# Fetching a second weight piece earlier, and one matrix product moved ahead of a group, in a fused retention and MLP kernel

## Chip, cores, metric

One core of a Trainium2 chip. The metric is the device time of one execution in microseconds (us). Several executions are timed; one of them is taken with the profiler, and its trace is what the views below are read from. The span in a profile (666.3 us for the kernel before) is about 1.7 us shorter than the time of the same execution.

## The reference, cut to what matters

```python
# attention: (batch 4, heads 8, seq 768, head_dim 64), retention with a decay per head
state = gamma * state + k[t] (outer) v[t]
y[t]  = scale * q[t] @ state
# bridge to x: (3072 tokens, 512), then
h = x @ w_in                      # (512, 2048)
g = np.maximum(0.01 * h, h)       # leaky relu
return g @ w_out                  # (2048, 512)
```

The weights arrive as float64 and the kernel converts them itself. The sequence is cut into six groups of 128 positions; a group with its 4 batches has 512 tokens, in two halves of 256 (batches 0 and 1, batches 2 and 3).

## The kernel before, where the change and the argument touch it

Each weight piece (512 KB) is loaded and converted by three activations on ScalarE (`powers`) and three operations on VectorE (`mantissas`). Loads go out on one queue, in this order:

```python
    load_qk(0, 0); load_v(0, 0)      # qk is 512 KB, v 256 KB
    load_qk(0, 1); load_v(0, 1)
    load_piece(0)
    load_qk(0, 2); load_v(0, 2)
    load_piece(1)
    load_piece(2)
    load_piece(3, words)
    # ... qk and v of batch 3, the k's, group 1
```

The first products (`direct`, tiles `d`) multiply x by pieces 0 to 3 as they become ready. TensorE executes this order:

```python
    values(0, 1)              # tiles yp
    score(0, 2)               # needs qk of batch 2; tiles ap
    keep_busy(3)              # three bf16 filler matmuls, tile idle
    next(steps)               # direct product on piece 0 (8 matmuls)
    next(steps)               # direct product on piece 1
    values(0, 2)
    # ... (order on TensorE; the loads and conversions between are cut)
```

Later, matrix products run in the Strassen-Winograd form: seven products of blocks instead of eight, each 8 matmuls, collected in four accumulators A to D:

```python
        which = [("M1", "A", 0, 0), ("M6", "B", 5, 5), ("M5", "C", 4, 4), ("M4", "D", 3, 6),
                 ("M2", "A", 2, 2), ("M7", "B", 1, 1), ("M3", "C", 6, 3)]
        for m, bank, sa, sb in which:
            # first use of a letter: psum.tile([128, 2, N], FP32, tag="ff", bufs=4)
            # ... 8 matmuls of weight block sa and x (sb < 4) or t (sb - 4)
            takes(m, ps)      # ScalarE or VectorE reads the accumulator
            yield
```

M1 and M2 of the hidden layer read only the first token half of x. The others need `differences(x, t)`, hence both halves. VectorE frees B with M7's add and C with M3's. PSUM, the memory in which matmuls accumulate, holds four `ff` tiles of one bank and two `att` tiles of two (`two_banks` in the code). The end of the start-up:

```python
    scored_later(2); scored_later(3)          # scores and masks of group 1
    last_sum(0); next_mantissas()
    products_in_turn(2)                       # reads, values, state of batches 2, 3
    next_powers(); run(steps, {})             # last direct product
    tokens_taken(1, 2, x1); tokens_taken(1, 3, x1)
    differences(x1, t1)
    state_taken(1, 2); state_taken(1, 3)
    run(hidden(1, 0, x1, t1, *parts[1][1:]),
        {0: [next_mantissas], 1: [lambda: differences(*parts[0][1:])],
         2: [next_powers], 3: [lambda: add_sums(1)]})
    # then output(0, ...), output(1, ...), hidden(0, u=1), ...
```

## Time and profile before

| | before |
|---|---|
| time, first three runs | 668.04, 668.18, 670.51 us |
| profiled span, mean granted clock of TensorE (PE) | 666.3 us, 1.000 |
| PE busy | 659.5 us, 99% |
| VectorE (DVE) busy, ScalarE (ACT) busy | 56%, 26% |
| PE's waits in the waits view, whole span | 3.5 us |

The granted clock is the share of TensorE's full clock that the profile shows as granted. With PE busy for 99% of the span, the change looks for its saving in PE's idle time, and every wait that the waits view lists lies in the first 42 us. A timeline line gives the start, the length, the engine, the source line, what it writes and reads, how many instructions are merged, and in brackets the idle time ahead with what ended it. The lines themselves stand in the prediction.

### The profile page before, as it was taken

The page shows a single profiled execution, that of the slowest core. Times are in us where ns is not written, and L with a number is a line of the kernel's source. Part 1 is how long each engine was busy: PE and PEld are TensorE (multiplying, and loading weights), DVE is VectorE, ACT ScalarE, POOL GpSimd, SP SyncE. Part 2 cuts the span into 40 slices and gives each one's busy share as a digit, 9 for nine tenths or more (in the row PEclk, how much of TensorE's full clock was granted, in tenths as well). Part 3 has the DMA queues.
Part 4 walks back from the last instruction along what each step waited for, and adds up shares of the span by engine and source line. Part 5 has one row for each costly group of instructions (what it writes and reads, how often), then busy time and mean ns, then how long its engine had stood idle before and what let it go on. Part 6 is the DMA issues. An engine that isn't in the chain of part 4 may idle for free.

```text
span 666.3 us, 10403 instructions
## 1 busy us (share of the span) xinstructions
PE 659.5 (99%) x4505; PEld 572.8 (86%) x4505; DVE 374.3 (56%) x570; ACT 176.0 (26%) x322; POOL 20.1 (3%) x22
## 2 busy tenths in 40 slices
PE   8999999999999999999999999999999999999998
PEld 4888888888888888888888888888888888888886
DVE  5789869889888676315543613563431444431342
ACT  4854555255261002211201311210221220221210
POOL 0000000000000111000000100100100000000000
PEclk9999999999999999999999999999999999999999
DMA  8930312312312453003002200301300001000001
GB/s 321 399 107 32 126 64 64 126 65 89 133 67 85 167 191 127 1 0 128 1 31 83 77 1 1 127 1 64 127 1 0 2 0 40 23 1 1 0 1 63
DMA packets 15757, 48.92 MB, mean 73 GB/s; under 512 B 1752, under 2 KB 2008, under 8 KB 15712
## 3 DMA queue, kind: packets, MB, share of 16 engines
q1 hardware_dynamic: 15696, 48.24, 20.2%
q8 instruction: 35, 0.57, 0.3%
q14 instruction: 10, 0.08, 0.0%
q10 hardware_dynamic: 16, 0.02, 0.0%
HBM read 41.97 MB, written 6.29 MB: 72 GB/s over the span
## 4 chain that ended last, share of the span: by engine, by line
PE 97%; DMA 1%; SPq 1%; DVE 1%; ACT 0%; issue 0%; DVEq 0%
PE B_o L412 12%; PE A_o L412 12%; PE C_o L412 12%; PE C_h L412 12%; PE B_h L412 12%; PE A_h L412 12%; PE D_o L412 6%; PE D_h L412 6%; PE yp L193 3%; PE ap L165 3%; PE d L434 2%; PE yp L184 2%; DMA raw<-in_weights_dram 1%; PE yp L208 1%; SPq L134 0%; PE sums L208 0%
## 5 line engine op out<-in xcount | busy, mean ns | idle before, releaser
L412 PE MATMUL A_h<-x,w 128*128 128x256 f32 x368 | 86.9, 379 | 0.0
L412 PEld LDWEIGHTS A_h<-x,w 128*128 128x128 f32 x368 | 69.9, 190 | 9.5
L412 PE MATMUL A_o<-g,w 128*128 128x256 f32 x288 | 68.0, 379 | 0.0
L447 ACT ACTIVATE g<-g 128x512 f32<-128x512 f32 x69 | 42.0, 630 | 91.3 <-DVE g L361 91.3
L412 PEld LDWEIGHTS A_o<-g,w 128*128 128x128 f32 x288 | 54.7, 190 | 7.4
L452 ACT COPY m<-A_h 128x512 f32<-128x512 f32 x23 | 13.4, 582 | 141.3 <-PE A_h L412 101.6
L361 DVE TENSOR_TENSOR m<-m,B_o 128x512 f32<-128x512 f32 x16 | 10.9, 684 | 63.9 <-PE B_o L412 63.9
L361 DVE TENSOR_TENSOR m<-m,B_h 128x512 f32<-128x512 f32 x23 | 15.7, 684 | 54.7 <-PE B_h L412 54.7
L412 PE MATMUL C_h<-t,w 128*128 128x256 f32 x184 | 44.1, 382 | 0.0
L412 PE MATMUL B_h<-x,w 128*128 128x256 f32 x184 | 44.1, 382 | 0.0
L412 PE MATMUL B_h<-t,w 128*128 128x256 f32 x184 | 43.5, 379 | 0.0
L412 PE MATMUL C_h<-x,w 128*128 128x256 f32 x184 | 43.5, 379 | 0.0
L412 PE MATMUL D_h<-t,w 128*128 128x256 f32 x184 | 43.5, 379 | 0.0
L238 DVE TENSOR_TENSOR x<-yp,dec 128x512 f32<-128x512 f32 x24 | 16.4, 687 | 48.0 <-PE yp L208 34.2
L412 PEld LDWEIGHTS C_h<-t,w 128*128 128x128 f32 x184 | 34.5, 190 | 5.5 <-issue 0.9
L412 PEld LDWEIGHTS B_h<-t,w 128*128 128x128 f32 x184 | 35.0, 190 | 4.8
L412 PEld LDWEIGHTS C_h<-x,w 128*128 128x128 f32 x184 | 35.0, 190 | 4.8
L412 PEld LDWEIGHTS D_h<-t,w 128*128 128x128 f32 x184 | 35.0, 190 | 4.8
L412 PEld LDWEIGHTS B_h<-x,w 128*128 128x128 f32 x184 | 34.5, 190 | 5.1 <-issue 0.3
L364 DVE TENSOR_TENSOR gd<-g,gd 128x512 f32<-128x512 f32 x48 | 35.5, 740 | 1.6
L170 DVE TENSOR_TENSOR am<-ap,mask 128x1024 f32<-128x1024 f32 x24 | 28.5, 1218 | 10.5 <-PE ap L165 10.5
L412 PE MATMUL B_o<-gd,w 128*128 128x256 f32 x144 | 34.0, 379 | 0.0
(118 smaller groups left out, 1020.4 us busy)
## 6 DMA issues: line engine op xcount, KB each, us to landing
raw<-in_weights_dram SPq DMA_DIRECT2D x31, 512.0 KB, 4.2
qk<-in_qk_dram SPq DMA_DIRECT2D x19, 512.0 KB, 3.8
kv<-in_kv_dram SPq DMA_DIRECT2D x17, 512.0 KB, 4.5
out_dram<-o SPq DMA_DIRECT2D x23, 256.0 KB, 2.1
in<-in_qk_dram SPq DMA_DIRECT2D x3, 512.0 KB, 7.7
in<-in_kv_dram SPq DMA_DIRECT2D x3, 512.0 KB, 8.2
kv<-in_kv_dram SPq DMA_DIRECT2D x4, 256.0 KB, 7.3
o_in<-in_qk_dram SPq DMA_DIRECT2D x2, 512.0 KB, 8.7
```

The costliest lines, as they stand in the source:

```text
L165: nc.tensor.matmul(ps[ts(u, 64), j, a, :], lhsT=x[ts(j, 64), 1, a, ts(u, 64)], rhs=x[ts(j, 64), 0, a, :])
L170: nc.vector.tensor_tensor(out=am.rearrange("p j a t -> p (j a) t"), in0=scores[c, b].rearrange("p j a t -> p (j a) t"), in1=mask.unsqueeze ...
L184: nc.tensor.matmul(ps[ts(i, 64), j, m, :], lhsT=st[b][ts(j, 64), a, :], rhs=x[ts(j, 64), 0, a, :], start=(m == 0), stop=False, skip_group_ ...
L193: nc.tensor.matmul(ps[ts(i, 64), j, m, :], lhsT=y[:, 1, 2 * a + j, :], rhs=am[:, j, a, :], start=(c == 0 and m == 0), stop=True, skip_grou ...
L208: nc.tensor.matmul(sp[ts(j, 64), a, :], lhsT=y[:, 0, 2 * a + j, :], rhs=y[:, 1, 2 * a + j, :], start=start, stop=True, skip_group_check=True)
L238: nc.vector.tensor_tensor(out=blocks, in0=ps[:, :, 0 : HP // 2, :], in1=gq, op=ALU.mult)
L361: nc.vector.tensor_tensor(out=out, in0=a, in1=b, op=ALU.add)
L364: nc.vector.tensor_tensor(out=out, in0=a, in1=b, op=ALU.subtract)
L412: nc.tensor.matmul(half, lhsT=block(w, sa)[:, k, ts(i, 128)], rhs=rhs[:, k, :], start=(first and (i == 0 or split) and n == 0 and k == 0), ...
L434: nc.tensor.matmul(banks[r][:, i, :], lhsT=block(2 * u, r + 2 * kh)[:, k, ts(i, 128)], rhs=x[:, 2 * kh + th, k, :], start=(step == 0 and i ...
L447: nc.scalar.activation(g[:, i], g[:, i], AF.Prelu, alpha=0.01)
L452: nc.scalar.copy(out=got["m1"], in_=ps)
```

## The change

The intent is to shorten PE's wait for the second weight piece, and to put work into the hole in which PE waits for a masked score tile.

```diff
     load_piece(0)
+    load_piece(1)
     load_qk(0, 2)
     load_v(0, 2)
-    load_piece(1)
...
-        for m, bank, sa, sb in which:
+        for m, bank, sa, sb in (which[i] for i in order):
...
     scored_later(2)
     scored_later(3)
+    later = hidden(1, 0, x1, t1, *parts[1][1:], order=(0, 4, 1, 2, 3, 5, 6))
+    next(later)
     last_sum(0)
...
-    run(hidden(1, 0, x1, t1, *parts[1][1:]),
-        {0: [next_mantissas], ...
+    run(later, {0: [next_mantissas], ...
```

I call the first hunk part 1 and the rest part 2. In part 2, M1 runs right behind the scores of group 1, and M2 is the first product of what is left.

More of the change, by code (lines that the diff above doesn't have):

```diff
@@ L387, in last_difference, with seven @@
         minus(x[:, 1], x[:, 3], x[:, 1])
-    def seven(tiles, name, takes, takes_half=None):
+    ORDER = (0, 1, 2, 3, 4, 5, 6)
+    def seven(tiles, name, takes, takes_half=None, order=ORDER):
         banks = {}
@@ L440, in direct, with hidden @@
             yield
-    def hidden(c, u, x, t, g, gd):
+    def hidden(c, u, x, t, g, gd, order=ORDER):
         got = {}
@@ L473, in takes @@
                 differences(g, gd)
-        return seven([(2 * u, x, t)], f"h{at}", takes)
+        return seven([(2 * u, x, t)], f"h{at}", takes, order=order)
     def output(c, o, parts, first, final):
@@ L732 @@
     state_taken(1, 3)
-    run(hidden(1, 0, x1, t1, *parts[1][1:]),
-        {0: [next_mantissas], 1: [lambda: differences(*parts[0][1:])],
-         2: [next_powers], 3: [lambda: add_sums(1)]})
+    run(later, {0: [next_mantissas], 1: [lambda: differences(*parts[0][1:])],
+                2: [next_powers], 3: [lambda: add_sums(1)]})
     for u in range(NU):
```

## The prediction

> **What bounds the kernel now.** I read the page first: the matmul engine (PE) is busy 99% of 666.3 us and the chain that ended last is 97% PE. So almost any microsecond taken from PE's idle time is a microsecond of the kernel, and there is very little of it. The second view, who waited for whom with the filter PE, lists all of it over the whole span:
>
> ```profile
> PE d L434 <- DVE w L357: 1.4, 2, 1.0
> PE idle L624 <- DVE t L619: 1.4, 1, 1.4
> PE yp L184 <- DVE am L170: 0.5, 1, 0.5
> PE ap L165 <- DMA qk<-in_qk_dram: 0.2, 1, 0.2
> ```
>
> The columns are total us, times, longest. The change aims at the first row (waits for converted weights) and the third (a wait for a masked score tile); together 1.9 us, 0.3% of the time. That caps the change before any detail. The third view, the timeline of PE in the first 50 us, shows where they lie:
>
> ```profile
> 11.33 1.10 PE L165 MATMUL ap<-o_in 64*64 64x128 f32 x32
> 12.37 0.82 PE L624 MATMUL idle<-t 128*128 128x512 bf16 x3
> 13.58 1.99 PE L434 MATMUL d<-x,w 128*128 128x256 f32 x8 [0.39 <-DVE w L357]
> 16.59 1.99 PE L434 MATMUL d<-x,w 128*128 128x256 f32 x8 [1.01 <-DVE w L357]
> ...
> 39.89 1.05 PE L165 MATMUL ap<-qk 64*64 64x128 f32 x32
> 41.41 0.67 PE L184 MATMUL yp<-in,states 64*64 64x128 f32 x16 [0.47 <-DVE am L170]
> ```
>
> The first number is the start, the second the length. The product on weight piece 1 starts at 16.59, 3.01 us after the one on piece 0, though eight matmuls occupy PE for only 1.92 us (the spacing 16.59 to 18.51). Why it waits is in the timelines of the other two engines:
>
> ```profile
> 13.22 0.66 ACT L334 ACTIVATE w<-raw 128x512 f32<-128x512 uint16 x1 [1.53 <-DMA raw<-in_weights_dram]
> ...
> 15.84 0.69 DVE L357 SCALAR_TENSOR_TENSOR w<-w,z 128x512 f32<-128x512 f32 x1
> ```
>
> ScalarE (ACT) sat idle from 11.69 until piece 1 landed at 13.22; three activations and three VectorE (DVE) operations later, at 16.53, the piece is usable.
>
> [...] from issue 11 on, the queue's own waits show each issue waiting for the landing of the one eight before it, so issue times read as landings: piece 0 at 9.69, qk of batch 2 near 10.97, its v at 11.87, piece 1 at 13.22; 512 KB per 1.28 us, 410 GB/s[...]. [...] the largest idle gap here is 1.4 us and the granted clock is 1.000, so moving a gap of 1 us should not cost clock. [...] The code uses four one-bank tiles (ff) and two two-bank tiles (att)[...]. A new accumulator must therefore wait for VectorE or ScalarE to empty an old one. That becomes my main term.
>
> **Part 1, piece 1 earlier.** Nothing is added or removed; piece 1 (512 KB) overtakes qk (512 KB) and v (256 KB) of batch 2. Estimated landings from the spacing above: piece 1 at 10.97, qk at 12.25, v at 13.2; everything later unchanged.
> - ScalarE goes straight from piece 0 to piece 1 at 11.7 (first activation over at 12.4, second at 13.06, third at 13.7). VectorE finishes piece 0 at 13.52 and needs about 1.95 us (14.58 to 16.53) for piece 1: ready at 15.5 instead of 16.53.
> - But PE's program has the score of batch 2 ahead of the first weight product. It began at 11.33; now it waits for qk until 12.3. It takes 1.04, and three filler matmuls take 0.64 (one alone lasts 0.39 at 9.82, three last 0.82, so each further one adds 0.215). So product 0 starts at 12.3 + 1.04 + 0.64 = 13.98, 0.4 later than before, and product 1 at 13.98 + 1.92 = 15.90.
> - Shift x = 16.59 - 15.90 = **0.69 us**. I checked the consumers down to 41 us: piece 2 (ready 18.9, used 19.9), piece 3 (23.0, used 24.7), decays and later loads (at least 0.7 us ahead of their use, and they aren't moved). I find none that gives x back.
>
> **Part 2, product M1 of hidden(1,0) ahead.** M1 needs only block 0 of the weights and x1[:,0] (first token half, written by 38.8). Its eight matmuls (1.73 us by the spacing in the chain, 47.58 to 49.31) move from after the last direct product to between the scores and the reads of batches 2 and 3. Scores stream 32 matmuls in 0.93 (38.96 to 39.89), so PE is free at 40.82 and the reads come at 41.41: the real hole is 0.59, a little over the 0.47 listed. M1 fills it wholly. M2 becomes the first product of the rest: it also reads only the first half, and it adds into M1's bank, long copied by then. The count of instructions is equal. So on PE alone the gain is 0.69 + 0.59 = **1.28 us**.
>
> **What comes back.** M1 is longer than its hole, so the products of batches 2 and 3 come 1.73 - 0.59 = 1.14 later in PE's order; with x, 0.45 later by the clock. VectorE's tokens_taken, which starts a long burst of work, waits for exactly those. It began at 45.24 and now begins near 45.69, while PE's later stream is 1.28 earlier. VectorE in that stretch, timeline of before:
>
> ```profile
> 45.24 1.29 DVE L238 TENSOR_TENSOR x<-yp,dec 128x512 f32<-128x512 f32 x2 [0.29 <-PE yp L208]
> ...
> 61.94 0.69 DVE L364 TENSOR_TENSOR gd<-g 128x512 f32<-128x512 f32 x1 [0.70 <-ACT g L447]
> ...
> 71.50 0.68 DVE L361 TENSOR_TENSOR m<-m,B_o 128x512 f32<-128x512 f32 x1
> ...
> 73.49 0.68 DVE L361 TENSOR_TENSOR o<-u,C_o 128x512 f32<-128x512 f32 x1
> 75.30 0.69 DVE L361 TENSOR_TENSOR u<-m,B_o 128x512 f32<-128x512 f32 x1 [1.14 <-PE B_o L412]
> ```
>
> From 45.24 to 74.2 it is 27.24 us busy in 29.00 (the table by stretch), and its one listed wait, 0.70 for ScalarE's leaky, follows from VectorE's own add before it. So I take this burst as rigid: all of it moves by +0.45. Its adds free the banks of output(0,0) for output(1,0):
> - B_o is free at 72.18 before, its next use began at 73.32: slack 1.14. Now free at 72.63, plus 0.06 (semaphore, as from 13.52 to 13.58): 72.69, against a wish for 73.32 - 1.28 = 72.04. Wait 0.65.
> - C_o is free at 74.17, next use 75.05: slack 0.88. Now 74.68, against 72.69 + 1.73 = 74.42. Wait 0.26.
> - After that VectorE has its 1.14 idle at 75.3 and over 2 us of slack to the next banks; no more waits.
> Net: 1.28 - 0.65 - 0.26 = **0.37 us**. The same falls out in one step: the end is set by VectorE's burst at C_o, 75.05 - 74.68. It also says that part 2 alone would lose: with x = 0 the release would be 1.14 later, the next use at 75.37, a loss of 0.32; and part 1 alone would gain its whole 0.69.
>
> **Time.** Before, two runs agree at 668.04 and 668.18 (one at 670.51 is an outlier); 668.11 - 0.37 = **667.7 us**.
>
> **Rivals.**
> - *No debt: both holes close and stay closed*, 666.8. For it: VectorE is busy only 56% overall[...]. Against: the burst has no gap before 75.3. It would be right if VectorE's order has slack that I can't see, or if the change moved a bank's release ahead.
> - *Part 1 gives nothing*, because qk of batch 2, overtaken, delays the score by as much as piece 1 gains. If qk landed at 12.9 or later, x is near 0 and the sum is -0.3: 668.4. For it: piece 1 is not used until the score is through. Against: 1.28 us per 512 KB is read off four landings in a row.
> - *Part 1 gives its most*: if qk lands by 11.9, conversion is the limit, x = 16.59 - 15.5 = 1.1, and the sum is 0.75: 667.4.
> - *Clock*: the gap before the score grows to 1 us; if the granted clock fell, some us would be lost. The trace had 1.01 at 15.5 with no fall, so I give it little.
>
> **Range and chances.** The rivals span 666.8 to 668.4, and two clean runs of one kernel lie 0.14 apart; I keep some room above for an outlier: 667.0 to 668.5. No rival comes near 2% (13.4 us), as all of PE's idle time in the profile is under 4 us. Within 2%: 0.99.
>
> **What the profile after would show.** Right: the activation on piece 1 starts near 11.7, the score of batch 2 near 12.3 with a wait for its qk, the products on pieces 0 and 1 near 14.0 and 15.9 with no hole between; no wait of PE for am at 41; A_h once near 40.2; tokens_taken near 45.7; and new waits of PE in output(1,0), near 72.7 for B_o and 74.7 for C_o, some 0.9 us in sum, with VectorE's 1.14 idle near 75 gone or smaller. Wrong: no waits there means that the burst isn't rigid (time near 666.8); a score much later than 12.3 or a piece 1 later than 11.7 means that the landings are wrong; any new wait after 80 us is one I have not seen.

## The result

Six runs of the changed kernel: 666.64, 666.80, 666.65, 670.16, 667.87 and 668.09, median 667.34 us; six of the kernel before, median 668.24. The ratio is 0.9988, with a 95% interval of 0.9965 to 1.0011. Ratios here are the mean time of one kernel's fast runs over that of the other's in the same rounds, so not quite the ratio of the medians. By the 2% rule the two are the same; whether the gain differs from zero, these runs do not say. The profiled run took 666.64 us, span 664.9.

PE's waits over the whole span of the changed kernel:

```profile
PE idle L626 <- DVE t L621: 1.4, 1, 1.4
PE ap L165 <- DVE x L238: 0.8, 1, 0.8
```

The waits for converted weights and for the masked tile are both gone. A new one of 0.8 stands ahead of the score of batch 2; its qk is what was moved back. The label names VectorE, but other profiles of this order, below, name the DMA of that qk. PE's timeline and that of ScalarE and VectorE at the places that the prediction named:

```profile
12.23 1.10 PE L165 MATMUL ap<-o_in 64*64 64x128 f32 x32 [0.79 <-DVE x L238]
13.27 0.82 PE L626 MATMUL idle<-t 128*128 128x512 bf16 x3
13.93 3.62 PE L436 MATMUL d<-x,w 128*128 128x256 f32 x16
17.47 1.09 PE L193 MATMUL yp<-am,o_in 128*64 128x128 f32 x16
...
39.84 1.99 PE L414 MATMUL A_h<-x,w 128*128 128x256 f32 x8
41.76 0.67 PE L184 MATMUL yp<-in,states 64*64 64x128 f32 x16
```

```profile
11.46 0.65 ACT L334 ACTIVATE w<-raw 128x512 f32<-128x512 uint16 x1
```

```profile
45.58 1.29 DVE L238 TENSOR_TENSOR x<-yp,dec 128x512 f32<-128x512 f32 x2 [1.65 <-PE yp L208]
...
71.93 0.68 DVE L361 TENSOR_TENSOR m<-m,B_o 128x512 f32<-128x512 f32 x1
```

```profile
71.94 1.89 PE L414 MATMUL B_o<-gd,w 128*128 128x256 f32 x8
73.66 1.89 PE L414 MATMUL C_o<-gd,w 128*128 128x256 f32 x8
```

Both direct products now run as one stream of sixteen matmuls from 13.93, and the value products of batch 2 start at 17.47 instead of 18.51. VectorE's burst runs as forecast: its start is 45.58 (45.69 was forecast), and M7's add is 0.43 later than before (71.50), where 0.45 was forecast. And yet PE starts B_o at 71.94 while that add, which reads the earlier B_o, has only begun at 71.93. B_o was at 73.32 before: PE is 1.38 us ahead and stays so.

### The profile page after: what moved, and what is told of

The parts are those of the page before. It is cut to its first block, busy times and chain, and to the rows that moved or that the text cites. A ratio compares the mean times of both kernels' runs of the same rounds, so it can differ in the third digit from the quotient of the medians.

```text
span 664.9 us, 10405 instructions
## 1 busy us (share of the span) xinstructions
PE 659.4 (99%) x4505; PEld 573.6 (86%) x4505; DVE 373.9 (56%) x570; ACT 175.8 (26%) x322; POOL 20.1 (3%) x22
## 4 chain that ended last, share of the span: by engine, by line
PE 99%; DMA 1%; DVE 0%; issue 0%
PE B_o L414 13%; PE A_o L414 13%; PE C_o L414 12%; PE C_h L414 12%; PE B_h L414 12%; PE A_h L414 12%; PE D_o L414 6%; PE D_h L414 6%; PE ap L165 4%; PE yp L193 4%; PE d L436 2%; PE yp L184 2%; PE yp L208 1%; DMA qk<-in_qk_dram 1%; PE sums L208 0%; PE idle L626 0%
## 5 line engine op out<-in xcount | busy, mean ns | idle before, releaser
L364 DVE TENSOR_TENSOR gd<-g,gd 128x512 f32<-128x512 f32 x48 | 37.1, 773 | 1.7
```

Of the source, the lines that this page charges most:

```text
L364: nc.vector.tensor_tensor(out=out, in0=a, in1=b, op=ALU.subtract)
```

## Experiments

The executions scatter by more than the effect, so nearly every verdict below rests on distances inside a trace.

### The changed kernel again

No edit.

> The changed kernel once more, beside the kernel before on the same chip, because its six runs so far scatter from 666.6 to 670.2 us. The profile showed PE's stream 1.38 us ahead of before from 72 us on, with no later wait. If that gain is real, undisturbed runs lie 1.2 to 1.5 us under undisturbed runs of before, and the profiled span is near 664.9 us again. If the single profile flattered it, the span is within 0.5 us of before's 666.3.

Measured: median 666.95 us against 668.13 for eleven runs of before; ratio 0.9985 (0.9970 to 1.0000). The profile fell on an execution of 667.72 us, span 666.0, mean clock 0.997. So the expected span did not come, and neither stated reason fits, since the stretch from the first score of the pair ahead of M1 (39.02) to the next hidden layer's A_h (83.39) is 44.37 us, as in the first profile (37.93 to 82.30). All that was lost was lost before 18.6 us. The table by stretch of this profile shows what; after the stretch and its length come the busy times with counts for PE, PE's weight loads, VectorE, ScalarE and GpSimd, then PE's granted clock, the DMA share and GB/s:

```profile
6.00:8.00 2.00, 1.65 (x16) 0.82 (x20) 1.81 (x3) 0.58 (x1) 0.00 (x0) 0.94 0.98 352
8.00:10.00 2.00, 2.00 (x36) 1.67 (x30) 0.61 (x1) 0.00 (x0) 1.04 (x1) 0.50 1.02 408
10.00:12.00 2.00, 1.75 (x22) 1.44 (x21) 1.25 (x3) 1.83 (x3) 0.00 (x0) 0.71 1.03 412
```

The clock was halved from about 7.75 to 11.16 us, for 3.4 us. Halved for 3.4 of 666 us is a mean of 0.997, so I read the other executions with 0.997 as the same event; that is inferred, as they left no trace. Sorted by this number, the runs are:

| mean clock | before | changed | difference |
|---|---|---|---|
| 0.999 or 1.000 | 667.81 (7 runs) | 666.72 (3) | 1.09 |
| 0.997 | 668.23 (3) | 667.90 (2) | 0.33 |

Within one cell the runs differ by up to 1.13 us (667.12 to 668.25), so the differences are rough. One run of before at 670.50 is left out; some 670 us runs at full clock come with several of the kernels, and I have no cause for them.

### Part 1 alone

```diff
     load_piece(0)
+    load_piece(1)
     load_qk(0, 2)
     load_v(0, 2)
-    load_piece(1)
```

> Part 1 alone: piece 1 fetched right behind piece 0, no product moved. The prediction on record: PE's stream 0.69 us ahead at the scores of group 1, kept to the end (span 665.6). The reading after the result: 1.04 us ahead (scores of group 1, batch 2, at 37.93 instead of 38.96), kept to the end (span 665.3), with the wait of 0.47 us for the masked tile still there, near 40.4.

Measured: ordinary runs from 667.11 to 667.39 us (one at 670.48), ratio 0.9994 (0.9976 to 1.0012); span 665.5, clock 1.000. PE's waits, then two lines of its timeline:

```profile
PE yp L184 <- DVE am L170: 0.5, 1, 0.5
PE yp L193 <- DVE am L170: 0.4, 1, 0.4
PE ap L165 <- DMA o_in<-in_qk_dram: 0.3, 1, 0.3
```

```profile
17.78 1.09 PE L193 MATMUL yp<-am,o_in 128*64 128x128 f32 x16
...
40.69 0.67 PE L184 MATMUL yp<-in,states 64*64 64x128 f32 x16 [0.47 <-DVE am L170]
```

The score waits for its qk by name, and the hole at the masked tile stays. The value products start 0.73 earlier than in the profile of before: near 0.69, short of my 1.04. The stretch from the scores (38.23) to the next A_h (82.95) is 44.72, that of before (38.96 to 83.68). What part 1 gains is kept.

### Part 2 alone, twice, and the kernel before again

```diff
     load_piece(0)
-    load_piece(1)
     load_qk(0, 2)
     load_v(0, 2)
+    load_piece(1)
```

(taken from the changed kernel.)

> Part 2 alone: M1 ahead, weights fetched as before. The prediction on record, with banks taken to pass on by name: VectorE's burst comes over 1 us later and PE waits for it in the second output; a loss of 0.32 us (span 666.6). The rival after the result, with banks handed on in the order in which they come free: a gain of 0.34 us (span 665.95), no wait of PE after 41 us, and the burst starting near 46.6.

> Part 2 alone once more, for a profile with the clock at 1.000 all through (the first fell in an execution whose clock went to one half from 7.7 to 11.2 us). If so: PE waits about 1 us for converted piece 1 near 16.6 as before the change, the scores of group 1 start near 39.0 (less where the weights land earlier), and M1 gives 0.34 us at the hole near 41: from the first of those scores to A_h of the next hidden layer 44.38 us instead of 44.72. If the clock is halved again, product 1 follows product 0 without a wait and the value products of batch 2 start near 18.56, as in the first.

> The kernel before once more, for the spread of its landings and its wait for piece 1. At full clock: a wait of about 1 us for converted piece 1, value products of batch 2 between 18 and 19 us, the hole of 0.47 at the masked tile. At halved clock (7.7 to 11.2 us): the first products are late themselves, the wait for piece 1 is gone, and the value products of batch 2 start near 18.56 all the same: before, the halved clock costs nothing.

Measured: the five timed runs of part 2 alone are 667.73, 667.10, 668.36, 666.91 and 666.80, ratio 0.9986 (0.9970 to 1.0003). Its first profile had the halved clock (span 666.0, 0.997; shares of 0.94, 0.50 and 0.71 in the three stretches above, as there). So it makes a pair with the second profile of the changed kernel: the two differ in nothing but part 1, and in both the clock was halved over the same stretch. PE of part 2 alone, and then of the whole change, both halved:

```profile
14.78 3.85 PE L436 MATMUL d<-x,w 128*128 128x256 f32 x16 [0.40 <-DVE w L357]
18.56 1.09 PE L193 MATMUL yp<-am,o_in 128*64 128x128 f32 x16
```

```profile
14.78 3.85 PE L436 MATMUL d<-x,w 128*128 128x256 f32 x16
18.57 1.09 PE L193 MATMUL yp<-am,o_in 128*64 128x128 f32 x16
```

With the clock halved, part 1 gains nothing in this pair: 18.56 and 18.57. The value products of batch 1 come late, VectorE takes them before it finishes piece 0, and it starts on piece 1 at 14.64 in both; by then the piece has long landed in either order (ScalarE began on it at 12.02 in the new order and, right at its landing, at 12.94 in the old).

The other two profiles had the full clock. PE of part 2 alone and of before:

```profile
16.71 1.99 PE L436 MATMUL d<-x,w 128*128 128x256 f32 x8 [0.64 <-DVE w L357]
18.64 1.09 PE L193 MATMUL yp<-am,o_in 128*64 128x128 f32 x16
```

```profile
16.33 1.99 PE L434 MATMUL d<-x,w 128*128 128x256 f32 x8 [0.71 <-DVE w L357]
18.25 1.09 PE L193 MATMUL yp<-am,o_in 128*64 128x128 f32 x16
```

The single runs took 667.80 us (part 2 alone) and 667.79 (before): no gain shows, as part 2 alone reached the scores 0.38 later (39.09 against 38.71), more than the 0.35 that it saves after them. What was expected of before at halved clock stays untested, since this profile had the full clock.

So the wait for piece 1 is real at full clock, but 0.64 to 1.01 us long, by how the loads land. Start of the value products of batch 2 at full clock: old order 18.51, 18.25, 18.64 (mean 18.47); new order 17.47, 17.78, and 17.70 and 17.33 in the two kernels of the next section (mean 17.57). By these starts **part 1 is worth 0.90 us at full clock**, with 0.5 to 1.3 between single executions. The timed runs at full clock in which these kernels first ran side by side, without those near 670, show less: part 1 alone 667.26 (five runs) against 667.81 for before, 0.55; part 2 alone 667.29 (four runs), 0.52. They scatter by more than these differ, so the size of part 1 is known to some tenths only.

Part 2 needs no mean. The ends of the stretch from the first of the two scores to the next A_h, in before and then in the changed kernel:

```profile
38.96 1.10 PE L165 MATMUL ap<-in 64*64 64x128 f32 x32
...
83.68 1.89 PE L412 MATMUL A_h<-x,w 128*128 128x256 f32 x8
```

```profile
37.93 1.10 PE L165 MATMUL ap<-in 64*64 64x128 f32 x32
...
82.30 1.89 PE L414 MATMUL A_h<-x,w 128*128 128x256 f32 x8
```

The seven profiles that bear on it give 44.72 (before), 44.71 (before again) and 44.72 (part 1 alone) without it, and 44.37 (twice with the whole change), 44.37 and 44.37 (twice alone) with it. **Part 2 is worth 0.35 us**, at either clock. The loss of 0.32 that the prediction foresaw for part 2 alone is refuted.

### Where the forecast waits went

The prediction gave 0.91 us back because B_o and C_o of the second output would wait for B_o and C_o of the first. That assumes that a letter gets the bank of its own letter before it. The built program names the bank of every tile (before and after have the same for these):

```
hidden(1,0):  A 1   B 2   C 3   D 0
output(0,0):  A 1   B 2   C 0   D 3
output(1,0):  A 3   B 1   C 2   D 0
```

B_o of the second output takes bank 1, that of A_o, which ScalarE had copied long before (by 67.55 in the changed kernel, against a start at 71.94); C_o takes that of B_o; D_o takes that of C_o. In these lists banks go on in the order in which they come free. Recomputed with these: in the profile of the changed kernel the tightest place is B_o of the *first* output, which takes B_h's bank. VectorE's add on B_h ran from 58.99 to 59.67 and PE started B_o at 59.85, 0.18 to spare:

```profile
58.99 0.68 DVE L361 TENSOR_TENSOR m<-m,B_h 128x512 f32<-128x512 f32 x1
```

```profile
59.85 1.89 PE L414 MATMUL B_o<-gd,w 128*128 128x256 f32 x8
```

So the rigid burst was no mistake, but the debt was not due. To test that, I made the burst longer:

```diff
+    def again(n):
+        _, g0, gd0 = parts[0]
+        for _ in range(n):
+            minus(gd0[:, 0], g0[:, 1], g0[:, 0])
-                1: [lambda: differences(*parts[0][1:])], ...
+                1: [lambda: again(1), lambda: differences(*parts[0][1:])], ...
```

and again(3) in the second kernel. The result is the same, since the subtraction is done over.

> The changed kernel with the first subtraction of the differences of parts[0] done once more (same result), which makes VectorE's burst 0.6 us longer. Banks handed on in the order in which they come free: the first tight place is B_o of the first output, which takes B_h's bank; in the changed kernel it had 0.18 us to spare, so PE waits there about 0.48 us (0.6 - 0.18 + 0.06), nowhere later, and the stretch from M2 of hidden(1,0) to A_h of the next hidden layer grows from 34.54 us by 0.48. Banks passed on by name, as the prediction had it: waits at B_o and C_o of both outputs, about 1.6 us in sum. Burst not rigid: no wait.

> The same with three more subtractions, 1.8 us. Order of release: one wait of about 1.7 us at B_o of the first output and none later; the stretch from M2 to A_h of the next hidden layer grows by 1.7 us. By name: waits in both outputs, some 2.8 us. Burst not rigid: under 1 us.

Measured, PE's waits after 60 us with one more subtraction, then with three:

```profile
PE B_o L414 <- DVE m L361: 0.4, 1, 0.4
```

```profile
PE B_o L414 <- DVE m L361: 1.9, 1, 1.9
```

One wait in each, at B_o of the first output (60.68 and 61.76), none later. With one, the burst up to M7's add of the hidden layer grew by 0.72 (13.41 to 14.13), and the stretch from M2 (47.99) to the next A_h (83.23) grew from 34.54 to 35.24, by 0.70: the 0.48 expected, 0.12 for a subtraction dearer than the 0.6 that I assumed, and 0.10 for a first group of matmuls that takes 1.83 instead of 1.73 after a wait. By name it would have been 1.6. B_o of the first output takes B_h's bank under either rule; what tells the rules apart is the size, and that neither C_o nor the second output waits.

With three, the burst grew by 2.2 us, but PE's stream lost 3.8: M2 starts at 47.62 and the next A_h at 86.00, 38.38 us later instead of 34.54. The expectation (1.7) is missed by more than the dearer subtractions. The table by stretch of this profile tells why:

```profile
60.00:62.00 2.00, 0.24 (x1) 0.24 (x2) 1.90 (x4) 0.00 (x0) 0.00 (x0) 1.00 0.00 0
62.00:64.00 2.00, 2.00 (x7) 1.64 (x7) 1.70 (x3) 1.46 (x3) 0.00 (x0) 0.67 0.00 0
64.00:66.00 2.00, 2.00 (x6) 1.61 (x5) 1.53 (x3) 1.97 (x4) 0.00 (x0) 0.50 0.00 0
```

PE sat idle for 1.90 us, and the clock was halved afterwards, from about 62.7 to 66.1. The next two groups of eight matmuls took 2.70 and 2.55 between starts instead of 1.73: 1.8 us more, as much again as the wait itself. The halving lasted 3.4 us in all three profiles that have one. The length of the wait ahead does not sort the cases: the clock was halved at 7.75 us in two profiles with a listed wait of only 0.35 or 0.32 us shortly ahead, though the kernels with one more subtraction and without the fillers (below) had waits of 1.58 and 1.60 us near 11 us and showed a granted clock of 1.00 there. What made it fall was not shown.

### Without the three fillers

```diff
     score(0, 2)
-    keep_busy(3)
     steps = direct(0, 0, x, parts[0][1], 0)
```

> The changed kernel without the three filler matmuls between the score of batch 2 and the product on piece 0. If the score, which waits for its late qk, is what holds the first two products, they start 0.3 us (product 0, then held by the conversion of piece 0 at 13.57) and 0.17 us (product 1, held by the conversion of piece 1 at 15.43) earlier, and the span falls by 0.17 us to about 664.7. If the fillers only fill time that is idle anyway, or if the clock falls without them, the span stays at 664.9 or rises.

Measured: 666.50 to 668.01, median 666.84, ratio 0.9981 (0.9967 to 0.9996); span 665.1.

```profile
12.72 1.10 PE L165 MATMUL ap<-o_in 64*64 64x128 f32 x32 [1.60 <-DMA o_in<-in_qk_dram]
13.90 3.86 PE L436 MATMUL d<-x,w 128*128 128x256 f32 x16
```

The score started 0.49 later than in the changed kernel's first profile, as its qk landed later (the issue that waits for it is at 12.60 instead of 12.11), and product 0 starts at the same time (13.90 against 13.93): 1.18 after the score instead of 1.70. What holds it now is the conversion of piece 0, as expected: VectorE's last operation on it runs from 13.15 to 13.84. So the fillers are on the path when the score waits, but the span did not fall as expected, and by the times this kernel can't be told from the changed one (666.95).

### Fillers where PE waited ahead of the halved clock

In both profiles with the early halving, PE had a wait of 0.35 or 0.32 us for the qk of batch 1 (at 7.5). I put two fillers there, in one kernel in place of the three later ones and in one beside them:

```diff
     decay_v(0, 0, nc.vector)
+    keep_busy(2)
     score(0, 1)
...
-    keep_busy(3)        # in the first of the two only
```

> The changed kernel with two fillers before the score of batch 1 (where PE waited 0.35 us for its qk in both executions whose clock was halved from 7.7 to 11.2 us) in place of the three after the score of batch 2. If that wait tips the clock, no execution has a mean clock of 0.997 (4 of 11 of the changed kernel had) and all ordinary runs lie near 666.6 us. If the clock falls for another cause, 0.997 is as frequent as before and those runs stay near 667.9 us. The fillers may put the first products off by up to 0.3 us where qk lands early.

> The same two fillers before the score of batch 1, and the three after the score of batch 2 kept: for the share of 0.997 executions once more, with as much filler as can be had without moving anything else. Same two outcomes; a little slower than the other (the three cost up to 0.3 us where the score waits for its qk).

Measured: none of the eleven executions has 0.997, where four of eleven of the changed kernel had. But those four are from other calls, and the kernel before, unchanged, had 0.997 in only one of eleven in this call against three of eleven in the earlier one. So these runs don't show that the fillers help. The times do not follow either: the first kernel has 666.53 and 666.62 but also three of 667.42 to 667.51 and a 670.65, ratio 1.0003 (0.9987 to 1.0020); the second 666.66 to 667.52, ratio 0.9989 (0.9978 to 1.0001). Both profiled spans are 664.9. So neither is a version that beats the changed kernel, and the halving is not the only scatter: at full clock the value products of batch 2 still start anywhere from 18.25 to 18.64 in the old order, 5.29 after ScalarE's start on the landed piece 1 (12.96 to 13.35) in each of its three profiles, and from 17.33 to 17.78 in the new one.

## Why the prediction was right, and where it was not

The time and the range held: 667.7 forecast, 667.34 the median. That was partly luck: the three runs from 666.64 to 666.80 lie below the range of 667.0 to 668.5, and the median fell into it because two executions with 0.997 and one of 670.16 stand above. At full clock the gain is over 1 us and not 0.37. Two errors in the sum, in x and in the hole, offset each other; a third, the debt to VectorE, did not.

- **The fetch**: the mechanism held. Activation on piece 1 at 11.46 (11.7 forecast, 13.22 before), score at 12.23 (12.3 forecast, 11.33 before) with a wait, product 0 at 13.93 (13.98), no hole behind it. The term x, 0.69, measured 0.90 at full clock. One reason is in the first profile: I let each product occupy PE for 1.92, a spacing read where a wait comes before and another kind of matmul follows. In a stream it is 1.73, so product 1 started near 15.66 and not at 15.90, and the value products at 17.47 and not at 17.82. The other is the spread of the landings.
- **The hole at the masked tile**: 0.59 forecast, 0.35 measured. M1 does fill it, but set among small tiles it takes 1.92 (39.84 to 41.76) instead of 1.73, with a change of tile shape at either end (its first spacing between matmuls is 0.32 and its last 0.31, the others 0.22), and the scores ahead stretch by 0.06. 0.59 - 0.19 - 0.06 is 0.34. A first spacing of 0.32 also follows a plain wait (at 16.59 in before), so the change of tile shape is not shown to be its cause.
- **What comes back**: this step failed. The burst was rigid and as late as forecast (0.43 against 0.45), but "B_o is free at 72.18 before, its next use began at 73.32" paired the wrong tiles, and so did the C_o line. Nothing comes back, and 0.91 us of the forecast's losses did not occur. The longer burst shows the real limit, at B_o of the first output, with 0.18 us to spare.
- **The rival "no debt"** (666.8) is what full-clock executions show: 666.48 to 666.95 us, but for one run at 670.16.
- **The clock**: "moving a gap of 1 us should not cost clock" was an estimate from one execution at 1.000, and it missed the point. The mean of 0.997, read as the halved clock, comes in some executions of either kernel (3 of 11 of before in one call), so it doesn't take the change. But there part 1 gains nothing, so the gain is about 1.1 in one kind of execution and 0.3 in the other. The median of 667.34 lies between the two because of that mix. The forecast gain of 0.37 was near what the halved executions show only by chance.

What stays open: the cause of the 670 us runs, what tips the early halving, and whether the changed order makes the halving more frequent (4 of 11 against 4 of 22 for before).

## What to carry to other kernels

Before you charge a wait for an accumulator, look up which bank the new tile really gets: with several buffers under one tag it need not be the one of the same name (here B_o got the bank of A_o), and the slack that counts is that of the bank's last reader (here 0.18 us, and a wait of 0.44 with one more subtraction). A product put into a hole among runs of another tile shape can cost more than its stream spacing (here 1.92 us instead of 1.73), so compare a stretch that begins and ends outside of the place. Where the start-up depends on landings and clock, an end-to-end time of a tenth of a per cent mixes several kinds of execution; sort them before you compare.
